# Soft-MoE weights behind attention: no dummy products in the last expert layer, finer release of weights' places, ten small products behind the last dispatch sum

## The chip, the cores and the metric

The kernel runs on one core of a Trainium2 chip. The metric is the device time of one execution in microseconds (us). Engines are named as the profile does: PE (TensorE's products; PEld its weight loads), DVE (VectorE), ACT (ScalarE), POOL (GpSimd), SP (SyncE, which issues the transfers here; SPq is its queue).

## The reference

Three layers stand behind each other, all in float32: attention with a memory term, a soft mixture of experts, and a feed-forward network. Only the second and the joint to the third matter here.

```python
x = attn_out.transpose(0, 2, 1, 3).reshape(B * S, H * D)     # 2304 tokens x 512
# soft mixture of experts: 8 experts, 4 slots each
logits = x @ phi                                             # 2304 x 32
d = softmax over tokens of logits                            # dispatch
slot_input = (d.T @ x).reshape(8, 4, 512)
for e in range(8):
    h = np.maximum(slot_input[e] @ w1[e], 0.0)               # w1[e]: 512 x 1024
    slot_out[e] = h @ w2[e]                                  # w2[e]: 1024 x 512
x = softmax over slots of logits @ slot_out                  # combine
# feed-forward: 512 -> 2048 -> 512
r = np.maximum(x @ w_in, 0.0)
out = (s * (r * r) + b) @ w_out
```

## The kernel before

The program has three stages. In the first, attention runs over 16 pairs of heads; the order of its parts is a hand-written table (`STEP`), and each batch of four pairs adds to the dispatch sum (`dispatch_sum`, L503, and `dispatch_add`, L515). While it runs, SP already loads expert weights into all the memory that is free.

The second stage is the experts. The last dispatch sum is followed by `merge`: a small product that spreads the common maximum (L537), an exponential and a multiplication (L539, L540: `sm`), a small product for the sums (L543), three small DVE steps up to the factors `sel` (L546), and four products that turn the summed tokens into slot inputs `slT` (L675, L676). Then come the expert layers in two groups of four experts: `layer1(0)`, `layer1(1)`, `layer2(0)` and, behind the combine weights, `layer2(1)`. Each product there is 32 columns wide: expert j of a group uses the strip of columns 32j to 32j+31, so that four products of different experts can run side by side. Layer 1 (L690) reads a 128 x 512 unit of `w1` for each of 4 x 2 x 4 steps, layer 2 (L706) a unit of `w2` for each of 8 x 4.

The two groups' weights are 128 units of 256 KB, 32 MB, more than there is room for. So places are used again: `load_next` requests the next weights for a place, and `used(n)` counts the units that are read and calls `load_next` for each place whose units are all done (L572). A place is two units wide in the pool `w`, or 2 to 7 units in memory that the first stage has given up (`R0`, `R1`, `R2`, `P` and others). All requests go into SP's one queue in the order of the calls; at most eight are under way, since each also waits for the landing of the eighth before it.

`layer2(1)` also has dummy products (L711): one 128 x 512 product behind each of the eight steps over `fc`, of the identity with the weights that were just read, into a scratch sum that nobody reads. Its real sum is taken out by ACT (`evac(so, acc)`, L714, recorded as L220), transposed (L717) and multiplied by `w_in` into the pieces of G (`g_piece`, L769 and L773).

The third stage runs `first` (L814 and steps on ACT and DVE) and `second` (L839 to L841, dense products) over all tokens. The output weights' first two requests (L192, into PT) wait for the last transposes of the combine weights (L753), the next one (into raw) for the last product of `layer2(1)`.

In the first stage, `warm(i)` puts small products (L216: identity with 64 columns of itself, as many as `T["wt"][i]` says) behind the parts of the last pair that the table `after` names.

Of the kernel before, what the change touches and what calls it, by code (L numbers as in the profile page):

```python
# [57 lines left out]
LEAST, MOST = struct.unpack("2f", struct.pack("2I", 896 << 20, 0x47EFFFFF))  # L58
TG = 384
T = dict(  # L60
    warm=1,
    wt=[3, 4, 4, 4, 3, 3],
    cp=['aaadaaadaaadaaad', 'aaadaaadaaadaaad', 'adadadadadadadad'],
    NB=4,
    sim=0,
# [26 lines left out]
def strided(ap, *dims):  # L92

    return bass.AP(ap.tensor, ap.offset, [list(ap.ap[0])] + [list(d) for d in dims])
# [3 lines left out]
def tile_attention_moe_ffn(  # L98
# [16 lines left out]
    PE, ACT, DVE, POOL, SP = nc.tensor, nc.scalar, nc.vector, nc.gpsimd, nc.sync  # L115
# [6 lines left out]
    ident = cs[:, L_ID:L_ID + 128]  # L122
# [30 lines left out]
    wt = {}  # L153
# [64 lines left out]
    def evac(dst, src, eng=None):  # L218
        if eng is None or eng == "n":
            nc.any.tensor_copy(dst, src)  # L220
        elif eng == "a":
            ACT.activation(out=dst, in_=src, func=AF.Copy)  # L222
        else:
            DVE.tensor_copy(dst, src)
# [340 lines left out]
    def load_next(place_of=None):  # L565

        n, tag = place_of or next(places, (0, None))
        if n and wnext[0] < len(wkeys):
            load_place(n, tag)
            held.append((wnext[0], n, tag))  # L570

    def used(n):  # L572
        freed[0] += n
        while held and held[0][0] <= freed[0]:
            _, n, tag = held.pop(0)
            if tag not in ONCE:
                load_next((n, tag))
# [23 lines left out]
    for name in SHARED:  # L601
# [1 line left out]
    batch = {  # L603
        "dx": (dispatch_exp, 0), "de": (dispatch_exp, 1), "dT": (dispatch_T, 0), "dU": (dispatch_T, 1),
        "gT": (slot_logits, 0), "gU": (slot_logits, 1), "ds": (dispatch_sum,), "du": (dispatch_add,)}
    after = {"V4": 0, "A": 1, "X": 2, "L": 3, "de": 4, "dT": 5}

    def part_of(name, p):
        if name in batch:
# [57 lines left out]
    def ps_h():  # L667
        return pH.tile([128, 512], F32, tag="h", name="h")

    def ps_y():  # L670
        return pY.tile([128, 512], F32, tag="y", name="y")
# [13 lines left out]
    def layer1(a):  # L685
        acc = [ps_y(), ps_y()]
        for kc in range(4):
            for fb in range(2):
                for j in range(4):
                    PE.matmul(  # L690
                        acc[fb][32 * j:32 * j + 32, :], slT[:, kc, :], wt["w1", a, kc, j, fb],
                        start=(kc == 0), stop=(kc == 3))
            used(8)
        for fb in range(2):
            ACT.activation(out=hs[:, fb * 512:(fb + 1) * 512], in_=acc[fb], func=AF.Relu)
        for g in range(2):
            t = ps_h()
            for i in range(4):
                PE.transpose(t[:, i * 128:(i + 1) * 128], hs[:, (4 * g + i) * 128:(4 * g + i + 1) * 128], ident)
            evac(hT[a][:, 4 * g:4 * g + 4, :], t.rearrange("p (i s) -> p i s", i=4))  # L700

    def layer2(a):
        acc = ps_y()
        for fc in range(8):
            for j in range(4):
                last_pe[0] = PE.matmul(  # L706
                    acc[32 * j:32 * j + 32, :], hT[a][:, fc, 32 * j:32 * j + 32], wt["w2", a, fc, j],
                    start=(fc == 0), stop=(fc == 7))
            if a == 1 and T["warm"]:
                for _ in range(T["warm"]):  # L710
                    PE.matmul(scratch, ident, wt["w2", a, fc, 0], start=True, stop=True)  # L711
            if fc % 2:
                used(8)
        evac(so, acc)  # L714
        t = ps_h()
        for dc in range(4):
            PE.transpose(t[:, dc * 128:(dc + 1) * 128], so[:, dc * 128:(dc + 1) * 128], ident)  # L717
        evac(sT[:, :, 16 * a:16 * a + 16].rearrange("p c (j s) -> p c j s", j=4),
             strided(t[:, 16 * a:16 * a + 1], (128, 4), (36, 4), (1, 4)))

    layer1(0)
    layer1(1)
    layer2(0)
    scratch = ps_y()


    XC = place("x", SIZE["x"], F32R)
# [3 lines left out]
    for b in range(B):  # L731
# [22 lines left out]
        evac(cT[:, b * S + 512:(b + 1) * S], t[:, 0:64])  # L754

    layer2(1)

    RC = [place(f"R{i}", SIZE[f"R{i}"], F32R) for i in range(3)]
# [167 lines left out]
```

## Time and profile before

| | |
|---|---|
| median of 3 runs | 505.52 us (504.72 to 506.94) |
| the profiled execution, its own time | 507.53 us |
| its span, first to last instruction | 505.7 us |
| mean granted clock of TensorE | 0.99 |
| PE busy | 478.2 us, 95% |
| DVE, ACT busy | 316.0 and 316.4 us |

The median is what the changed kernel's time is set against. The profiled execution is another, single run; all times of views below count from its first instruction. The granted clock is a share of 2.4 GHz: 1.00 is that, 0.50 is 1.2 GHz.

### The profile page before, as it was taken

The page shows a single profiled execution, that of the slowest core. Times are in us where ns is not written, and L with a number is a line of the kernel's source. Part 1 is how long each engine was busy: PE and PEld are TensorE (multiplying, and loading weights), DVE is VectorE, ACT ScalarE, POOL GpSimd, SP SyncE. Part 2 cuts the span into 40 slices and gives each one's busy share as a digit, 9 for nine tenths or more (in the row PEclk, how much of TensorE's full clock was granted, in tenths as well). Part 3 has the DMA queues.
Part 4 walks back from the last instruction along what each step waited for, and adds up shares of the span by engine and source line. Part 5 has one row for each costly group of instructions (what it writes and reads, how often), then busy time and mean ns, then how long its engine had stood idle before and what let it go on. Part 6 is the DMA issues. An engine that isn't in the chain of part 4 may idle for free.

```text
span 505.7 us, 12512 instructions
## 1 busy us (share of the span) xinstructions
PE 478.2 (95%) x5043; PEld 347.3 (69%) x5043; DVE 316.0 (62%) x830; ACT 316.4 (63%) x611; POOL 47.3 (9%) x90
## 2 busy tenths in 40 slices
PE   6989998979998999889997999999999999999997
PEld 3667676757676768633322578878888888888885
DVE  3869786949796977500604899873654645545451
ACT  3968685848685956103205999996755655556552
POOL 3230404130403041000000000000000000000000
PEclk9999999989999999979999999999999999999999
DMA  8883746453746464989982334200300100100001
GB/s 249 246 248 102 224 147 182 160 166 107 220 149 179 168 234 162 393 300 387 387 310 83 106 145 167 84 0 1 125 2 0 62 1 0 64 0 33 31 1 62
DMA packets 40281, 71.91 MB, mean 142 GB/s; under 512 B 4000, under 2 KB 16800, under 8 KB 40224
## 3 DMA queue, kind: packets, MB, share of 16 engines
q1 hardware_dynamic: 39072, 70.51, 41.3%
q8 instruction: 40, 0.66, 0.5%
q10 hardware_dynamic: 1152, 0.60, 0.5%
q14 instruction: 17, 0.14, 0.1%
HBM read 66.38 MB, written 4.72 MB: 141 GB/s over the span
## 4 chain that ended last, share of the span: by engine, by line
PE 89%; ACT 5%; issue 3%; DVE 2%; DMA 1%; DVEq 0%; ACTq 0%
PE y L841 13%; PE y L839 13%; PE y L840 13%; PE s L401 10%; PE s L370 8%; PE s L323 8%; PE y L706 4%; PE h L814 3%; PE y L690 3%; ACT P L361 2%; PE s L386 2%; PE y L711 2%; PE s L336 2%; PE s L439 1%; ACT PT L222 1%
## 5 line engine op out<-in xcount | busy, mean ns | idle before, releaser
L841 PE MATMUL y<-w,R 128*128 128x512 f32 x288 | 113.9, 395 | 0.0
L840 PE MATMUL y<-w,R 128*128 128x512 f32 x288 | 113.8, 395 | 0.0
L839 PE MATMUL y<-w,R 128*128 128x512 f32 x288 | 112.9, 394 | 0.9 <-ACT R L822 0.9
L361 ACT ACTIVATE P<-P,st 128x384 f32<-128x384 f32 (+3 forms) x144 | 75.8, 577 | 16.3 <-DVE st L345 15.6
L818 ACT ACTIVATE P<-h 128x384 f32<-128x384 f32 x96 | 46.7, 488 | 56.3 <-PE h L814 56.1
L823 DVE TENSOR_TENSOR R<-P,R 128x384 fp32r<-128x384 f32 x56 | 31.1, 556 | 68.3 <-ACT R L822 68.2
L222 ACT ACTIVATE PT<-s 128x768 f32<-128x768 f32 (+1 forms) x64 | 50.3, 819 | 31.5 <-PE s L370 31.4
L345 DVE CUSTOM_DVE_ANT_0 P<-s,cs 128x384 f32<-128x384 f32 (+3 forms) x128 | 57.2, 485 | 13.3 <-PE s L323 12.9
L839 PEld LDWEIGHTS y<-w,R 128*128 128x128 f32 x288 | 54.0, 188 | 16.2 <-ACT R L822 1.8
L841 PEld LDWEIGHTS y<-w,R 128*128 128x128 f32 x288 | 54.1, 188 | 13.4 <-issue 0.5
L840 PEld LDWEIGHTS y<-w,R 128*128 128x128 f32 x288 | 54.0, 188 | 9.1 <-issue 0.2
L370 PE MATMUL s<-cs,P 128*128 128x128 f32 x392 | 51.6, 278 | 1.3 <-ACT PT L222 0.8
L370 PEld LDWEIGHTS s<-cs,P 128*128 128x128 f32 x392 | 41.9, 141 | 12.3 <-issue 7.6
L821 ACT ACTIVATE P<-P,sbt 128x384 f32<-128x384 f32 x56 | 39.8, 710 | 1.5
L814 PE MATMUL h<-x,R 128*128 128x384 f32 x96 | 33.3, 349 | 0.6 <-ACT P L818 0.6
L401 PE MATMUL s<-raw,PT 128*64 128x65 f32 x768 | 28.3, 229 | 4.7 <-issue 4.7
L401 PE MATMUL s<-Q,PT 128*64 128x65 f32 x768 | 28.6, 224 | 4.4 <-issue 4.4
L401 PEld LDWEIGHTS s<-Q,PT 128*64 128x64 f32 x768 | 24.9, 137 | 11.0 <-issue 9.9
L433 POOL TENSOR_TENSOR x<-x,R 128x512 f32<-128x512 f32 (+1 forms) x15 | 21.1, 1409 | 120.0 <-DVE R L419 88.8
L401 PEld LDWEIGHTS s<-raw,PT 128*64 128x64 f32 x768 | 25.3, 142 | 9.7 <-issue 9.1
L820 ACT ACTIVATE P<-P 128x384 f32<-128x384 f32 x56 | 29.5, 526 | 1.5
L822 ACT ACTIVATE R<-P 128x384 fp32r<-128x384 f32 x56 | 29.4, 524 | 1.3
(192 smaller groups left out, 659.2 us busy)
## 6 DMA issues: line engine op xcount, KB each, us to landing
w<-in_w_dram SPq DMA_DIRECT2D x37, 512.0 KB, 6.5
raw<-in_w_in_dram SPq DMA_DIRECT2D x8, 1024.0 KB, 5.2
R<-in_qk_dram SPq DMA_DIRECT2D x32, 144.0 KB, 3.9
out_dram<-P SPq DMA_DIRECT2D x18, 256.0 KB, 2.1
raw<-in_w_out_dram SPq DMA_DIRECT2D x4, 1024.0 KB, 4.9
R<-in_w_dram SPq DMA_DIRECT2D x6, 512.0 KB, 8.9
P<-in_w_dram SPq DMA_DIRECT2D x6, 512.0 KB, 9.0
PT<-in_w_out_dram SPq DMA_DIRECT2D x3, 1024.0 KB, 4.9
```

The source lines that it names most:

```text
L222: ACT.activation(out=dst, in_=src, func=AF.Copy)
L323: PE.matmul(s_t[p, t][h][HALF[a], :], q[r, t * 128 + 64 * a:t * 128 + 64 * a + 64], k[r, 0:n], start=True, stop=True)
L345: DVE.tensor_tensor_reduce(out=Pt[t][:, n * h:n * h + n], in0=s_t[p, t][h], in1=cs[:, L_END - n:L_END], scale=-0.125, scalar=BIG, op0=ALU. ...
L361: ACT.activation(out=pt, in_=pt, func=AF.Exp, scale=-1.0, bias=st[:, c:c + 1])
L370: PE.transpose(tp[:, j * 128:(j + 1) * 128], PA[:, c:c + 128], ident)
L401: PE.matmul(o[HALF[a], 512 * h + 65 * t:512 * h + 65 * t + 65], PT[t][:, c + 64 * a:c + 64 * a + 64], v[:, v0:v0 + 65], start=(kb == 0), s ...
L814: PE.matmul(hp[:, 0:TG], G(k * 128, 128), cT[:, g * TG:(g + 1) * TG], start=True, stop=True)
L818: ACT.activation(out=r, in_=hp[:, 0:TG], func=AF.Relu)
L821: ACT.activation(out=r, in_=r, func=AF.Identity, scale=sbt[:, 0:1], bias=sbt[:, 1:2])
L839: PE.matmul(acc[g, i], hi[:, c], who[k], start=(k == 0), stop=False)
L840: PE.matmul(acc[g, i], hi[:, c], wlo[k], start=False, stop=False)
L841: PE.matmul(acc[g, i], lo[:, c], who[k], start=False, stop=(k == NK - 1))
```

## The change

Three edits. The dummy products of `layer2(1)` and their scratch sum go. `used(8)` behind each full step becomes `used(2)` behind each pair of units. And `warm` gets a seventh entry: ten small products behind the last pair's `ds`, which is `dispatch_sum` with `merge(1)` (the product L537) at its end.

```diff
 T = dict(
-    warm=1,
-    wt=[3, 4, 4, 4, 3, 3],
+    wt=[3, 4, 4, 4, 3, 3, 10],
...
-    after = {"V4": 0, "A": 1, "X": 2, "L": 3, "de": 4, "dT": 5}
+    after = {"V4": 0, "A": 1, "X": 2, "L": 3, "de": 4, "dT": 5, "ds": 6}
...
                         start=(kc == 0), stop=(kc == 3))
-            used(8)
+                    if fb:
+                        used(2)
...
-            if a == 1 and T["warm"]:
-                for _ in range(T["warm"]):
-                    PE.matmul(scratch, ident, wt["w2", a, fc, 0], start=True, stop=True)
-            if fc % 2:
-                used(8)
+                if fc % 2:
+                    used(2)
...
-    scratch = ps_y()
```

**First place**, on PE, from the last dispatch sum to the first expert layer (s and h are sums in PSUM, Es the dispatch weights, M's row the maxima, cs the constants with the identity). Before:

```order
L506 MATMUL s<-x,Es 32x512 x4
L510 MATMUL s<-x,Es 32x128 x4
L537 MATMUL s<-cs,M 128x1
L543 MATMUL s<-sm,cs 128x1
L675 MATMUL h<-sel,uacc 128x32 x4
```

and now, with line numbers one lower:

```order
L505 MATMUL s<-x,Es 32x512 x4
L509 MATMUL s<-x,Es 32x128 x4
L536 MATMUL s<-cs,M 128x1
L215 MATMUL s<-cs 128x64 x10
L542 MATMUL s<-sm,cs 128x1
L674 MATMUL h<-sel,uacc 128x32 x4
```

The ten products stand between the product of the maxima and the product of the sums, in PE's queue ahead of the latter.

**Second place**, on PE, the last half of `layer2(1)` (y is its sum; w, R and P are places of weights, raw the hidden values; the row with the dummies has cs, the identity). Before:

```order
L711 MATMUL y<-R_3459,cs 128x512
L711 MATMUL y<-R_3470,cs 128x512
L706 MATMUL y<-R_3470,raw 32x512
L706 MATMUL y<-P,raw 32x512 x2
L706 MATMUL y<-R_3470,raw 32x512 x2
L706 MATMUL y<-P,raw 32x512 x4
L711 MATMUL y<-P,cs 128x512 x2
L706 MATMUL y<-R_3517,raw 32x512
L706 MATMUL y<-w,raw 32x512
L706 MATMUL y<-P,raw 32x512
L706 MATMUL y<-R_3517,raw 32x512 x2
L706 MATMUL y<-w,raw 32x512
```

and now:

```order
L706 MATMUL y<-R_3480,raw 32x512
L706 MATMUL y<-P,raw 32x512 x2
L706 MATMUL y<-R_3480,raw 32x512 x2
L706 MATMUL y<-P,raw 32x512 x4
L706 MATMUL y<-R_3528,raw 32x512
L706 MATMUL y<-w,raw 32x512
L706 MATMUL y<-P,raw 32x512
L706 MATMUL y<-R_3528,raw 32x512 x2
L706 MATMUL y<-w,raw 32x512
```

The real products stand in the same order, without the dummies between them; the same holds for the four dummies further ahead.

**Third place**, on SP, the first requests for used places in layer 1, with the semaphores that each waits for (DMAHW: an earlier landing; PE: a product). Before:

```order
L173 DMA M<-in_w_dram 128x2x512 [waits DMAHW1_49,PE_49,Activation_49]
L173 DMA w<-in_w_dram 128x2x512 [waits DMAHW2_49,PE_49]
L173 DMA w<-in_w_dram 128x2x512 [waits DMAHW3_49,PE_49]
L173 DMA w<-in_w_dram 128x2x512 [waits DMAHW4_49,PE_49]
L173 DMA w<-in_w_dram 128x2x512 [waits DMAHW5_49,PE_49]
```

and now:

```order
L172 DMA M<-in_w_dram 128x2x512 [waits DMAHW1_49,PE_49,Activation_49]
L172 DMA w<-in_w_dram 128x2x512 [waits DMAHW2_49,PE_49]
L172 DMA w<-in_w_dram 128x2x512 [waits DMAHW3_49,PE_49]
L172 DMA w<-in_w_dram 128x2x512 [waits DMAHW4_49,PE_49]
L172 DMA w<-in_w_dram 128x2x512 [waits DMAHW5_49,PE_49]
```

Nothing moved here, nor in the rest of SP's 216 rows.

## Rows read from the trace of the kernel before

**Rows 1.** The page: busy time of each engine.

```profile
PE 478.2 (95%) x5043; PEld 347.3 (69%) x5043; DVE 316.0 (62%) x830; ACT 316.4 (63%) x611; POOL 47.3 (9%) x90
```

**Rows 2.** Windows: length, PE, PEld, DVE, ACT, POOL busy, clock, DMA share, GB/s.

```profile
210.00:215.00 5.00, 4.14 (x38) 2.70 (x36) 2.05 (x9) 2.25 (x11) 0.00 (x0) 1.00 1.01 394
215.00:220.00 5.00, 3.58 (x17) 2.18 (x20) 1.07 (x5) 0.00 (x0) 0.00 (x0) 0.54 1.05 390
220.00:225.00 5.00, 5.00 (x40) 1.31 (x36) 0.00 (x0) 0.00 (x0) 0.00 (x0) 0.77 0.53 152
225.00:230.00 5.00, 5.00 (x52) 1.44 (x48) 0.00 (x0) 0.00 (x0) 0.00 (x0) 1.00 1.05 400
...
260.00:262.00 2.00, 2.00 (x16) 0.47 (x15) 0.00 (x0) 0.00 (x0) 0.00 (x0) 1.00 1.03 402
262.00:264.00 2.00, 2.00 (x10) 0.76 (x12) 0.00 (x0) 0.00 (x0) 0.00 (x0) 1.00 0.44 170
264.00:270.00 6.00, 6.00 (x34) 1.55 (x28) 0.00 (x0) 0.00 (x0) 0.00 (x0) 1.00 0.00 1
270.00:275.00 5.00, 3.60 (x34) 1.93 (x33) 3.14 (x7) 3.42 (x9) 0.00 (x0) 1.00 0.63 210
...
280.00:285.00 5.00, 5.00 (x24) 2.71 (x23) 3.93 (x6) 4.95 (x9) 0.00 (x0) 1.00 0.40 162
```

**Rows 3.** Chain of waits, 246 to 283: shares by line; start, us, what.

```profile
by line: PE y L706 34.1%; PE y L711 21.8%; PE h L750 5.1%; PE h L773 4.2%; ACT raw L220 3.8%; PE h L717 3.6%; PE y L839 3.2%; issue 3.0%; ACT P L820 2.8%; ACT P L818 2.7%; PE h L769 2.4%; PE h L753 2.2%; PE y L841 1.9%; PE h L814 1.9%; PE y
...
262.01 1.91 PE y L711 x4
...
266.61 1.91 PE y L711 x4
268.53 1.89 PE y L706 x12
...
270.50 0.59 ACT raw L220
```

**Rows 4.** SP's last two weight requests: issue (start) and us to landing.

```profile
L173 SPq DMA_DIRECT2D R<-in_w_dram x1: 378/378/378, 252.0 to 252.0; - x1
...
DMA to landing us min/median/max: 8.8/8.8/8.8
L173 SPq DMA_DIRECT2D w<-in_w_dram x1: 379/379/379, 252.8 to 252.8; - x1
...
DMA to landing us min/median/max: 9.4/9.4/9.4
```

**Rows 5.** Timeline, 202 to 226: start, length, engine, line, operation, records [idle before].

```profile
208.82 0.97 PEld L216 LDWEIGHTS s<-cs 128*128 128x128 f32 x8
...
209.88 0.75 PEld L216 LDWEIGHTS s<-cs 128*128 128x128 f32 x6
...
213.49 0.38 PE L537 MATMUL s<-cs,M 1*128 1x1 f32 x2
...
214.43 0.16 DVE L540 TENSOR_TENSOR sm<-sm,ssum 128x1 f32<-128x1 f32 x1 [0.36 <-ACT sm L539]
...
214.64 0.38 PE L543 MATMUL s<-sm,cs 128*128 128x1 f32 x2 [0.77 <-DVE sm L540]
...
215.99 1.89 PE L675 MATMUL h<-sel,uacc 128*128 128x32 f32 x8 [0.97 <-DVE sel L546]
...
218.33 8.14 PE L690 MATMUL y<-w,slT 128*32 128x512 f32 x56 [0.45 <-DVE slT L676]
219.19 0.20 PEld L690 LDWEIGHTS y<-w,slT 128*32 128x32 f32 x4 [0.66 <-issue]
220.04 0.20 PEld L690 LDWEIGHTS y<-w,slT 128*32 128x32 f32 x4 [0.66 <-issue]
...
221.98 4.21 SPq L173 DMA_DIRECT2D w<-in_w_dram  x8
...
222.87 0.12 PEld L690 LDWEIGHTS y<-w,slT 128*32 128x32 f32 x4 [0.31 <-issue]
```

## Prediction

> **What bounds the kernel now.** The page comes first: TensorE is busy for 95% of the span [rows 1], so time is won or lost on PE, and only where PE's work is not needed or comes too late. Stage by stage [rows 2], the reader is to look at two columns, the granted clock and the DMA share. Up to 262 the transfers run at a full share (1.03 in 260 to 262), with one hole, 220 to 225, where the share is 0.53. Behind 264 they stand still (0.00 in 264 to 270) while PE is 100% busy: there PE alone decides. The clock is at 1.00 (the 2.4 GHz level) everywhere here but in two rows: mean 0.54 in 215 to 220 and 0.77 in 220 to 225, a spell at 1.2 GHz.
>
> The chain of waits says what PE does behind 246 [rows 3]: of the 37 us from 246 to 283, 21.8% are the dummy products of L711, 8.07 us. They are on the chain itself. The last ones run from 262.01 (1.91 us, two dummies) and from 266.61 (1.91 us, two more), then comes the last piece of the second expert layer, 1.89 us from 268.53, and at 270.50 ACT takes the sum out.
>
> What would PE wait for if they were gone? The weights' requests [rows 4]: the last one leaves SP at 252.8 and lands 9.4 us later, at 262.2; the one before it leaves at 252.0 and lands after 8.8, at 260.8.
>
> **Edit 1, no dummies.** PE's own work would end at 270.42 - 8.07 = 262.35 if no weight were late. But the last weights (the last w of the order) land at 262.2, and two of the last six products read them. In the new order [the change, second place] these six are the same that make up the last piece of the chain, 12 records (a product stands as two in the trace: L675's four are x8 there) in 1.89 us [rows 3]. The second of the six waits for the last landing, the four behind it stand in PE's queue, the sixth reads the same weights in the same strip of columns. So the layer ends between 262.2 + 1.7 (two products of one strip behind each other, of 2 x 0.43 us each by the spacing of L690's records [rows 5]) and 262.2 + 1.9 (the whole piece); I take 264.1. ACT's evacuation moves from 270.50 to 264.2: **-6.3 us**. The first 1.8 us of the dummies' 8.07 are thus lost to a new wait, for weights. The bound above is the whole 8.07 (no wait at all), the bound below is the clock's (rivals). What comes next does not depend on an absolute time: the output weights' first two requests are out before the layer's end, the next one waits for this layer's last product, so it moves along; and from 280 PE is fully busy again [rows 2].
>
> **Edit 2, places given back by two units.** Here I reckon 0. A request waits for the product that last read its place, not for the call that gives the place back; the call only says where the request stands in SP's queue. SP's order is the same row by row, its waits too [the change, third place], and in the built program each of these waits stands on the same product as before (its count is ten higher for the ten new ones). Above 0 it could only cost if a request were moved past another; none is. The order also swaps three small DVE rows in the combine weights (a reduction to 5 columns, two casts), which I take as free too: DVE has nothing at all to do in 260 to 270 [rows 2], so whatever they delay is caught up before PE's last weights are there.
>
> **Edit 3, ten small products behind the last dispatch sum.** They stand between L537 and L543 on PE [the change, first place]. Their price: four such products took 0.97 us of weight loads, three took 0.75 [rows 5], so 0.245 us each and 2.45 us for ten. L537 ends at 213.87, so they run to 216.3. L543 started at 214.64, held by DVE's sm (L540, to 214.59); now it waits for PE until about 216.35: 1.7 us later, and behind it in a row the three DVE steps to sel, the slot products L675 and all of layer 1. This is the new cost. What it may buy is the clock: L675 took 1.89 us and the first groups of four records of L690 came 0.85 us apart (219.19 to 220.04) against 0.43 later (0.31 idle and 0.12 busy at 222.87) [rows 5], the two levels of the clock. The first weight request behind the hole waits for the fifth product of L690 and left at 221.98.
> - If the clock holds: L675 starts at 217.65 and takes 0.95, L690 starts at 218.33 + 1.7 - 0.95 = 219.1, and the fifth product ends half of (221.98 - 218.33) = 1.8 us later, at 220.9: the request leaves **1.1 us earlier**.
> - If the clock falls just when L690 starts: 219.1 + 3.65 = 222.7, **0.8 us later**.
>
> Before the clock fell, PE had only L543 and L675 to do from 213.87 to 218.33, 4.5 us; now that thin stretch runs from 216.3 to 219.1, 2.8 us, with ten products ahead of it. No row says on which side it falls. The middle of the two is -0.15; I take **-0.3 us**, nearer to the gain, since the stretch is the shorter one (range -1.1 to +0.8). From 225 on, the stream runs at a full share (1.05 in 225 to 230) [rows 2], so it moves as a whole and the last landing with it; the hole (47% of 5 us, 2.3 us) leaves room for that. If the request leaves 0.8 later, the end of edit 1 goes to 264.9.
>
> **The sum.** -6.3 + 0 - 0.3 = -6.6 us. The profiled execution took 507.53 us itself (505.7 of span and 1.8 around it), which would go to 500.9. It was 2.0 us above the median of the runs, 505.52; from the median the forecast is **498.9 us**.
>
> **The rivals.**
> - *The clock falls while PE waits for the last weights.* For: behind 256 PE, without dummies, has one lone product (a quarter of the columns) per landing and then waits about a microsecond for the next; the trace shows such a fall after thin work, 215 to 222. Against: PE kept the clock in 270 to 275 with 3.60 us busy of 5, and in 210 to 215 with 4.14 [rows 2]. Price: the last piece goes from 1.89 to 3.7 (+1.8), and the pieces of G behind it, PE's 3.60 us of 270 to 275, take up to 3.6 more; much of that stretch is a chain through ACT, so I take +2.6. That leaves 6.6 - 4.4 = 2.2 of the gain: **503.3 us**.
> - The Trainium skill, in "TensorE: Matmul & The Clock Gate", section "HAM oscillation — how this bites in real kernels", says that a kernel whose bursts of products are shorter than the waits for transfers between them is throttled anew at each wait. By that rule this rival's 503.3 is the time and not 498.9. The fall at 215 agrees with the rule in kind (work too thin), but no run here shows PE waiting in bursts for weights.
> - *Slower.* The same fall, but the clock stays at 1.2 GHz into the second layer's dense products. To end more than 2.5 us above before it must cost 6.6 + 2.5 = 9.1: 1.8 + 3.6 = 5.4 up to there, and 3.7 more, so the dense products (5.00 us busy of 5 in 280 to 285) must stay slow for 7.4 us. Place: from 273 to 281 of the new run. That gives **508.1 us**. Against: L690 began at 218.33 at 1.2 GHz, and the mean of 0.77 over 220 to 225 says that only 2.3 us of these were slow, so that dense work brought the clock back at 222.3, 4 us after its start [rows 2, 5].
> - *The dummies were hidden anyway.* If PE had to wait for weights as long as the dummies took, nothing but edit 3 would remain: **505.2 us**. Against: the landing at 262.2 and the idle transfers from 264 on. It would need a stream that ends 6 us later than before.
>
> **How the numbers follow.** The forecast has 0.60, the fallen clock 0.28, the slower one 0.05, the hidden dummies 0.07. The forecast's own range is 497.0 (the stream 1.1 earlier, and a microsecond for the spread of the runs) to 501.0 (0.8 later and the same spread). To leave out no more than 2 in 10 the range must take in most of the fallen clock: **497.0 to 504.6**. Half a per cent, 2.5 us, is about what a measurement of this kernel tells from no change; faster means below 503.0. All of the forecast and half of the fallen clock lie there: 0.74. Slower 0.05, the rest, 0.21, is no change.
>
> **What would show it.** Right: no rows of L711; DMA full until about 262, ACT's evacuation of the sum (L220 behind L706) at 264 instead of 270.5, directly behind the last landing; idle time on PE named by weights in 256 to 262; the span 6 to 7 us shorter and every stretch behind 270 unchanged in length. For edit 3, L543 at about 216.3, and the first w request of L173 at 221 or at 222.7, according to the clock in 216 to 222. For edit 2, the requests in the same order. Wrong: a granted clock below 1.00 anywhere in 256 to 280, with the pieces of G stretched; or the last weights landing later than 263.

## The result, and the profile after

The changed kernel took **501.5 us** (median of 20 runs, 496.5 to 506.7). The kernel before, run in the same set, took 508.12 us there (20 runs, 504.1 to 514.7). The ratio is **0.9889, 95% interval 0.9862 to 0.9916**: 1.1% faster, and of the 505.52 us of the three runs shown it makes 499.9 us, 5.6 us less. The forecast was 6.6 us less. The ratios and intervals in this document leave out each kernel's slow runs, those more than 1.5% above its fastest (three of the changed kernel's 20 here), so they are not quotients of the medians beside them, which would give 0.987 here.

The profiled execution is one that TensorE's clock disturbed early: it took 506.7 us, with three falls of the clock in the first stage. So spans are not compared here but stretches, counted from the end of the product of the maxima, the last product ahead of the place of the ten new ones. It is L537 in the kernel before and L536 in the changed one, whose lines are numbered one lower; below it is called L537 for every kernel. The page's first line for the changed kernel answers to [rows 1] (a product is two records: 16 of the dummies are gone, 20 of the ten small products have come, 5043 to 5047):

```profile
PE 475.3 (94%) x5047; PEld 349.1 (69%) x5047; DVE 315.9 (63%) x830; ACT 316.4 (63%) x611; POOL 47.2 (9%) x90
```

The windows of the changed kernel, 218 to 275, answer to [rows 2] (its L537 ends at 217.84 and not at 213.87, so these lie some 4 us later):

```profile
218.00:222.00 4.00, 3.12 (x29) 3.07 (x28) 1.48 (x6) 0.65 (x3) 0.00 (x0) 0.99 1.05 387
222.00:225.00 3.00, 2.55 (x15) 0.99 (x18) 0.29 (x1) 0.00 (x0) 0.00 (x0) 0.50 0.92 337
225.00:230.00 5.00, 5.00 (x32) 1.15 (x28) 0.00 (x0) 0.00 (x0) 0.00 (x0) 0.62 0.43 123
230.00:235.00 5.00, 5.00 (x52) 1.43 (x48) 0.00 (x0) 0.00 (x0) 0.00 (x0) 1.00 1.04 395
255.00:260.00 5.00, 4.91 (x27) 1.94 (x25) 3.06 (x10) 1.65 (x5) 0.00 (x0) 1.00 1.05 387
...
264.00:267.20 3.20, 1.96 (x6) 0.14 (x2) 0.00 (x0) 0.00 (x0) 0.00 (x0) 1.00 1.02 396
267.20:269.20 2.00, 1.90 (x10) 0.38 (x10) 0.00 (x0) 0.00 (x0) 0.00 (x0) 1.00 0.22 86
269.20:275.00 5.80, 3.89 (x36) 2.32 (x36) 4.40 (x9) 4.57 (x13) 0.00 (x0) 1.00 0.51 181
```

Read them from the bottom. The transfers run at a full share until 267.2 and PE's last piece ends 2 us later; the six microseconds of [rows 2] in which the transfers stood still while PE was 100% busy are gone. In 264 to 267.2 PE is busy for 1.96 of 3.20 us, and the clock is 1.00 all the same. Further up, the clock is low for some 7 us: 0.50 over the 3 us from 222, and 0.62 over the next 5, so 3.8 of these. It fell at 222, behind the ten products and 1 us ahead of the start of the first expert layer (222.98 in the chain below).

The chain of waits of the changed kernel, 217 to 270, answers to [rows 3]:

```profile
217.54 0.31 PE s L536 x2
217.84 2.37 PE s L215 x20
...
221.27 1.28 PE h L674 x8
222.64 0.30 DVE slT L675
222.98 13.15 PE y L689 x93
236.13 10.78 DMA w<-in_w_dram
246.98 10.75 DMA R<-in_w_dram
257.79 9.38 DMA w<-in_w_dram
267.21 1.92 PE y L706 x10
269.21 0.59 ACT raw L219
```

The dummies' place on the chain has been taken by transfers: three requests, each waiting for an earlier one's landing, the last of them out at 257.79 and landed 9.38 us later, at 267.17. PE starts its last piece 0.04 behind that, and ACT takes the sum out 2.04 behind it. The timeline of the changed kernel names the new wait (start, length, engine, line, records, in brackets the idle time and its releaser):

```profile
265.86 1.04 PE L706 MATMUL y<-R,raw 128*32 128x512 f32 x2 [0.95 <-DMA R<-in_w_dram]
267.21 0.62 PE L706 MATMUL y<-w,raw 128*32 128x512 f32 x1 [0.31 <-DMA w<-in_w_dram]
```

The first used place is requested at 226.63 in the same timeline, 8.79 us behind L537; before it was 8.11 [rows 5]:

```profile
226.63 5.29 SPq L172 DMA_DIRECT2D w<-in_w_dram  x9
```

So the path from L537 to ACT's evacuation is 269.21 - 217.84 = 51.37 us, against 270.50 - 213.87 = 56.63 before: 5.26 less. The span fell by only 0.8 us (505.74 to 504.94), because L537 itself came 3.97 us later in this execution and the stretch behind the evacuation was 0.48 longer; 3.97 - 5.26 + 0.48 = -0.81.

### The profile page after: what moved, and what is told of

The parts are those of the page before. It is cut to its first block, busy times and chain, and to the rows that moved or that the text cites. A ratio compares the mean times of both kernels' runs of the same rounds, so it can differ in the third digit from the quotient of the medians.

```text
span 504.9 us, 12520 instructions
## 1 busy us (share of the span) xinstructions
PE 475.3 (94%) x5047; PEld 349.1 (69%) x5047; DVE 315.9 (63%) x830; ACT 316.4 (63%) x611; POOL 47.2 (9%) x90
## 4 chain that ended last, share of the span: by engine, by line
PE 80%; DMA 8%; ACT 5%; issue 3%; DVE 2%; DVEq 0%; ACTq 0%; SPq 0%
PE y L837 13%; PE y L835 12%; PE y L836 12%; PE s L400 10%; PE s L369 8%; PE s L322 8%; DMA w<-in_w_dram 4%; PE h L810 3%; PE y L689 3%; DMA R<-in_w_dram 2%; ACT P L360 2%; PE s L385 2%; PE s L335 2%; PE s L438 1%; DMA raw<-in_w_out_dram 1%
## 5 line engine op out<-in xcount | busy, mean ns | idle before, releaser
L400 PE MATMUL s<-Q,PT 128*64 128x65 f32 x768 | 29.8, 230 | 5.0 <-issue 5.0
L400 PEld LDWEIGHTS s<-Q,PT 128*64 128x64 f32 x768 | 26.1, 142 | 11.8 <-issue 10.7
```

The source lines that it names most:

```text
L400: PE.matmul(o[HALF[a], 512 * h + 65 * t:512 * h + 65 * t + 65], PT[t][:, c + 64 * a:c + 64 * a + 64], v[:, v0:v0 + 65], start=(kb == 0), s ...
```

## The experiments

My theory after the result: edit 1 (no dummies) is the whole gain; edit 2 (finer release) is nothing; edit 3 (the ten products) costs, since they come ahead of the sums' product and the clock falls anyway. The rivals: edit 3 buys clock and edit 1 gives less than it seems; or edit 2 moves something that the order doesn't show. Runs in one set share one chip and its runs of the kernel before; there were three sets. The first held no_dummies, ten_alone, by_two_alone and fitted (median of before 507.17), the second two_dummies, fewer_weights, changed_again and fitted_again (506.97), the third no_dummies_again, changed_third, fitted_third and full_width (506.90). Ratios are compared within a set; the rows of the table below come from all three.

A single table carries the traces, one profiled execution per row. Each number is a difference of two rows of that execution's timeline: from the end of L537 to the first weight request for a used place (**request**), to the landing of the last weights (**landing**), from there to ACT's evacuation of the second layer's sum (**behind**), and the whole of it (**path**); then L537's own end, and the stretch from the evacuation to the end of the span (**rest**). All in us.

| kernel, execution | request | landing | behind | path | L537 ends | rest |
|---|---|---|---|---|---|---|
| before | 8.11 | 48.32 | 8.31 | 56.63 | 213.87 | 235.25 |
| by_two_alone | 8.12 | 48.71 | 8.00 | 56.71 | 215.75 | 234.85 |
| ten_alone | 8.98 | 49.42 | 8.80 | 58.22 | 209.93 | 235.69 |
| two_dummies | 7.19 | 47.56 | 19.05 | 66.61 | 213.27 | 236.37 |
| no_dummies | 7.17 | 48.33 | 2.04 | 50.36 | 211.23 | 234.87 |
| no_dummies_again | 7.15 | 47.69 | 2.04 | 49.73 | 212.53 | 236.25 |
| the change | 8.79 | 49.33 | 2.04 | 51.37 | 217.84 | 235.73 |
| changed_again | 8.47 | 49.00 | 2.04 | 51.03 | 212.79 | 236.29 |
| changed_third | 8.08 | 48.54 | 2.04 | 50.58 | 212.61 | 234.86 |
| full_width | 7.85 | 48.24 | 2.04 | 50.28 | 219.33 | 235.53 |
| fitted | 5.56 | 46.47 | 2.04 | 48.51 | 212.05 | 234.86 |
| fitted_again | 5.56 | 46.84 | 2.04 | 48.88 | 217.80 | 236.37 |
| fitted_third | 5.56 | 45.94 | 2.04 | 47.98 | 212.23 | 234.86 |
| fewer_weights | 9.24 | 44.18 | 3.76 | 47.93 | 213.80 | 239.55 |

**Edit 1 alone** (no_dummies, no_dummies_again). Against the changed kernel:

```diff
-    wt=[3, 4, 4, 4, 3, 3, 10],
+    wt=[3, 4, 4, 4, 3, 3],
...
-    after = {"V4": 0, "A": 1, "X": 2, "L": 3, "de": 4, "dT": 5, "ds": 6}
+    after = {"V4": 0, "A": 1, "X": 2, "L": 3, "de": 4, "dT": 5}
...
-                    if fb:
-                        used(2)
+            used(8)
...
-                if fc % 2:
-                    used(2)
+            if fc % 2:
+                used(8)
```

> Edit 1 alone: the eight dummy products go, the rest is as before. My theory: the layer ends 1.9 us behind the last weights' landing, ACT takes the sum out 2.0 to 2.1 us behind that landing (8.3 before), so this edit is nearly the whole gain: -6.3 us, ratio 0.9875, and PE has idle time named by weights. Rival, the clock falls while PE waits for weights: a granted clock below 1.00 between the last landing and the first second-layer product, and only 2 us gained, ratio 0.996. Rival, the ten small products carry the change: nothing gained here.

> Edit 1 alone once more, beside the change and the fitted products on one chip. By the traces so far the last weights land 47.6 to 48.7 us behind the product of the maxima in kernels without the ten products and 49.0 to 49.4 with them. Theory: edit 1 alone is about 1 us faster than the whole change. Rival: the ten products gain in runs that were not profiled, the whole change is as fast or faster.

Measured: 499.2 us, ratio 0.984 (0.9786 to 0.9895); the second time 502.24 us, 0.9922 (0.9894 to 0.995). The chain of waits of no_dummies ends as that of the whole change does, with the last weights:

```profile
250.14 9.41 DMA w<-in_w_dram
...
259.60 1.92 PE y L705 x10
...
261.59 0.59 ACT raw L219
```

In the traces, behind goes from 8.31 and 8.00 to 2.04 both times, and the mean path from 56.67 (before and by_two_alone) to 50.05: -6.6 us. Of these, 6.1 stand in behind; the other 0.5 is an earlier landing, in executions where the clock stayed low for some 3 us around the start of the first layer and not for some 7. So edit 1 is the gain. But the two ratios of one and the same kernel hardly meet; a pair of medians does not tell this kernel from the whole change, whose ratios lie between them.

**The ten products alone** (ten_alone) and **the finer release alone** (by_two_alone). Against before:

```diff
-    wt=[3, 4, 4, 4, 3, 3],
+    wt=[3, 4, 4, 4, 3, 3, 10],
...
-    after = {"V4": 0, "A": 1, "X": 2, "L": 3, "de": 4, "dT": 5}
+    after = {"V4": 0, "A": 1, "X": 2, "L": 3, "de": 4, "dT": 5, "ds": 6}
```

```diff
-            used(8)
+                    if fb:
+                        used(2)
...
-            if fc % 2:
-                used(8)
+                if fc % 2:
+                    used(2)
```

> Edit 3 alone: ten small products behind the last dispatch sum, dummies stay. Theory: 2.4 us of products, L543 1.7 us later; the first weight request leaves 9.1 us behind the end of the product of the maxima if the clock falls at the start of the expert layers (8.4 before) and 7.3 if it holds. The end of the layer is then set by PE's dummies, not by the weights, so the whole moves with the start of layer 1: between 1 us earlier and 1 us later, ratio 0.998 to 1.002. Rival, the products keep the clock and are worth it: faster by over 0.3%. Rival, pure delay: 1.7 us slower, 1.0034.

> Edit 2 alone: places given back by two units. Theory: the same instructions in the same order with the same waits, so ratio 1.000, and what it differs from 1.000 is what this measurement tells of noise. Rival, earlier requests: the hole behind the last request of the first stage is shorter and the stream ends earlier, up to 2 us.

Measured: 508.21 us, ratio 1.0015 (0.9975 to 1.0055), and 508.48 us, 1.0015 (0.9974 to 1.0056). The finer release leaves the order of the instructions as it was, so its ratio is also a measurement of nothing: half a per cent either way is what these runs can't tell. (The three DVE rows that the prediction puts under edit 2 belong to edit 1: DVE's 830 instructions stand in the old order in by_two_alone and in the new one in no_dummies.) The ten products lie within that too; only the trace shows their price. The windows of ten_alone from 210 (its L537 ends at 209.93):

```profile
210.00:214.00 4.00, 3.12 (x28) 3.07 (x28) 1.57 (x6) 0.65 (x3) 0.00 (x0) 0.98 1.04 388
214.00:220.00 6.00, 5.55 (x28) 1.85 (x32) 0.29 (x1) 0.00 (x0) 0.00 (x0) 0.50 0.61 214
220.00:225.00 5.00, 5.00 (x48) 1.40 (x44) 0.00 (x0) 0.00 (x0) 0.00 (x0) 0.93 0.98 336
```

The clock holds through the ten products, is low for the whole of 214 to 220, on the second half of the slot products and the first expert layer, and is back before 221. Over the four executions with the ten products (ten_alone and the three of the change) the last landing lies 49.07 us behind L537 in the mean (48.54 to 49.42), over the five without them or a substitute (before, by_two_alone, two_dummies, and the two without dummies) 48.12 (47.56 to 48.71): by these means the edit costs 0.95 us. The ranges touch, since the clock's low spell at this place was short (some 3 us) in some executions of either group and long (some 7) in others. At equal spells they part: with a short one the request leaves 8.47 and 8.08 behind L537 with the ten products against 7.15 to 7.19 without, with a long one 8.98 and 8.79 against 8.11 and 8.12. That is 1.1 and 0.8 later in the mean.

**Two dummies per step** (two_dummies), against before:

```diff
-    warm=1,
+    warm=2,
```

> The kernel before with two dummy products behind each step instead of one. Theory: from the second half of the layer on the dummies are on the path one behind the other, 1.0 us each, so eight more push ACT's evacuation from 8.3 us behind the last landing to 15.5 to 16.5 us. Rival, dummies run in time in which PE would wait anyway: under 2 us more.

Measured: 518.03 us, one run, 11.1 above the median of 506.97 before. Behind grows from 8.31 to 19.05, by 10.7 us, where eight more dummies at the price of the first eight would be 8.07. The chain of waits of two_dummies, at its end, says why:

```profile
275.92 0.98 PE y L706 x2
276.90 1.06 PE y L711 x2
277.95 1.85 PE y L706 x10
...
279.88 0.59 ACT raw L220
```

A lone real product with a dummy on each side takes 0.98, while the five products of the last piece (ten records) take 1.85 together. So a dummy costs its own time and also pulls apart products that would have run side by side. Nothing swallowed any of the added time: the layer's end was on the path as read. This kernel and the next, fewer_weights, were run once each, so their totals have no interval.

**Fewer weights** (fewer_weights). The loads of the last eight units of `w2` are left out, and the second group's last two steps multiply with the weights of two steps earlier; the work on PE is the same. Against the changed kernel:

```diff
+    wkeys = wkeys[:-8]
...
-                    acc[32 * j:32 * j + 32, :], hT[a][:, fc, 32 * j:32 * j + 32], wt["w2", a, fc, j],
+                    acc[32 * j:32 * j + 32, :], hT[a][:, fc, 32 * j:32 * j + 32], wt["w2", a, fc - 2 if a and fc > 5 else fc, j],
```

> The changed kernel without the last eight units of the second experts' weights: they are not requested, and the last two steps of the last layer multiply with the weights of the two steps ahead of them, so the output is another. Theory, the end of the layer waits for the last landing alone: the stream ends five requests and 5.4 us earlier, and the layer's end follows until PE's own work binds, so ACT takes the sum out 3 to 4 us earlier, counted from the first weight request (42.6 us in the profiled run of the change, 39 to 39.5 here), and at 3.5 to 4.5 us behind the last landing instead of 2.0. Rival, PE's own products bind already: counted from the request no change.

Measured: 503.15 us, one run, with behind at 3.76: the layer ends 3.76 behind its last landing, not 2. From the request to the evacuation it is 47.93 - 9.24 = 38.7 us, against 42.6 in the changed kernel and 48.5 before. So the weights cost the changed kernel 3.9 us, and PE's own work without dummies is 9.8 us shorter by these executions, not 8.07. The total did not follow: rest is 239.55, against 234.9 to 236.4 everywhere else, some 3 to 5 us more. The windows of fewer_weights show one part of it:

```profile
260.00:265.00 5.00, 3.22 (x37) 1.21 (x27) 3.15 (x7) 2.88 (x6) 0.00 (x0) 1.00 0.43 147
265.00:270.00 5.00, 4.37 (x20) 2.31 (x24) 3.37 (x7) 3.31 (x10) 0.00 (x0) 0.52 0.51 170
270.00:275.00 5.00, 4.83 (x16) 2.49 (x8) 1.12 (x2) 4.92 (x8) 0.00 (x0) 0.50 0.30 124
```

The clock falls to the 1.2 GHz level at 265, behind the evacuation at 261.7, in the pieces of G, and stays there until 275. The other part stands in its chain of waits, which goes past the layer's end, through the first output weights (PT):

```profile
255.86 0.22 PE h L750
256.10 4.88 DMA PT<-in_w_out_dram
261.00 0.69 ACT Q L201
...
264.09 0.05 ACT w L799
...
264.62 0.27 ACT raw L222
```

Their request waits for the last transposes of the combine weights (L750), which this experiment leaves where they were (the request is 33.1 us behind the first weight request, 33.5 in the changed kernel). With the layer's end nearer to them, ACT takes out the first piece of G (L222) behind a step of their decoding (L799): 2.89 us behind the evacuation of the layer's sum, against 2.09 in changed_third. So the output weights are the next wait behind the experts' weights, and an earlier end of the layer alone would not be paid back in full. How much of the 3 to 5 us is this and how much the clock, this one execution doesn't part.

**Two products that fit the gaps** (fitted, fitted_again, fitted_third). The ten products are replaced by one of 352 columns behind `ds` and one of 448 behind `du`, where PE waits for DVE anyway. Against the changed kernel, from which the ten go:

```diff
+    FIT = {"ds": 352, "du": 448}
...
+        if p == NPAIR - 1 and name in FIT:
+            PE.matmul(bank_pair()[:, 0:FIT[name]], ident, cs[:, 0:FIT[name]], start=True, stop=True)
```

> As changed, but for the ten small products: one product of 352 columns behind the product of the maxima and one of 448 behind the product of the sums, each in a stretch where PE waits anyway (0.77 and 0.97 us). Theory: no delay on the way to layer 1, and the full-width products hold the clock through the first expert products more often; the first weight request leaves 6.2 to 6.6 us behind the end of the product of the maxima if it holds (8.4 before, 9.1 in the profiled run of the change), 8.4 if it does not. Against the kernel before -6.3 to -8.1 us, ratio 0.984 to 0.9875. Rival, the clock falls all the same: the gain is edit 1's alone, 0.9875.

> The fitted products once more beside the change on one chip. Theory: the request leaves 5.6 to 6.6 us behind the product of the maxima, so the whole is 1.5 to 3 us faster than the changed kernel, ratio to before 0.982 to 0.985. Rival, the clock does not hold in other runs: the same time as the changed kernel within half a per cent, with a request 8 us behind.

> The fitted products, third look. Theory: the last landing 46.4 to 46.9 us behind the product of the maxima, 2.4 us ahead of the change, so 0.3 to 0.6% faster than it. Rival: within 0.2% of the change.

Measured: 499.57, 499.51 and 501.17 us; ratios 0.9843 (0.9783 to 0.9903), 0.9842 (0.9794 to 0.9889) and 0.9821 (0.9782 to 0.986). The timeline of PE in fitted:

```profile
211.67 0.38 PE L536 MATMUL s<-cs,M 1*128 1x1 f32 x2
211.98 0.86 PE L620 MATMUL s<-cs 128*128 128x352 f32 x2
212.82 0.38 PE L542 MATMUL s<-sm,cs 128*128 128x1 f32 x2
213.07 1.00 PE L620 MATMUL s<-cs 128*128 128x448 f32 x2
214.18 1.05 PE L678 MATMUL h<-sel,uacc 128*128 128x32 f32 x8
215.68 6.64 PE L693 MATMUL y<-w,slT 128*32 128x512 f32 x60 [0.45 <-DVE slT L679]
```

The product of the sums (L542) starts 0.77 behind the end of L537 (212.05), as in the kernel before, where it was 0.77 too [rows 5]; the slot products start 0.11 behind the second filler. The first expert layer starts 3.63 us behind L537, exactly as in no_dummies: the fillers delay nothing. Then the clock, in the windows of fitted:

```profile
215.00:220.00 5.00, 4.55 (x44) 1.45 (x47) 0.29 (x1) 0.00 (x0) 0.00 (x0) 1.00 1.03 363
220.00:225.00 5.00, 5.00 (x52) 1.56 (x48) 0.00 (x0) 0.00 (x0) 0.00 (x0) 1.00 1.03 381
```

It stays at 1.00, the hole in the transfers is gone (1.03 and 1.03), and the request leaves 5.56 behind L537 in all three executions, 2.5 to 3.2 us earlier than in the change. The last landing comes 46.4 us behind L537 in the mean, 2.5 before that of the change (49.0) and 1.6 before that of edit 1 alone (48.0). The totals do not show this gain clear of the noise. In the one set that held all three kernels, fitted's interval (0.9782 to 0.986) lies clear of those of no_dummies_again and changed_third (0.9894 upward), but it rests on the three fastest of its six runs; the median of all six, 501.17 us, is only 0.2% under those two (502.24 and 501.95). In the other two sets the intervals overlap, and in the first, fitted and edit 1 alone have the same ratio (0.9843 and 0.984).

**Wide products in one place** (full_width): three products of 512, 512 and 384 columns where the ten stood.

```diff
+    FIT = {"ds": (512, 512, 384)}
```

> As changed, but the ten products of 64 columns are three of 512, 512 and 384 columns in the same place, 2.35 us against 2.37: the same delay with PE's columns full. If the ten were too thin to hold the clock, it holds here, L690's first request leaves 7.0 to 7.4 us behind the product of the maxima and the last weights land at 48 us. If the empty stretch behind them brings the clock down whatever they are, the request leaves at 8.5 to 9.2 and the landing is at 49.0 to 49.4.

Measured: 502.01 us, ratio 0.9875 (0.9835 to 0.9915). This one settles little: in the execution profiled, the clock had already fallen, eleven microseconds ahead of L537's end, and then it fell once more. The windows of full_width (L537 ends at 219.33):

```profile
210.00:215.00 5.00, 5.00 (x44) 4.68 (x45) 1.39 (x6) 1.01 (x5) 0.00 (x0) 0.50 1.04 407
215.00:220.00 5.00, 5.00 (x31) 3.06 (x31) 1.12 (x6) 1.01 (x5) 0.00 (x0) 0.65 1.05 390
220.00:225.00 5.00, 3.67 (x23) 2.21 (x25) 1.62 (x6) 0.23 (x2) 0.00 (x0) 1.00 0.49 176
225.00:230.00 5.00, 5.00 (x40) 1.29 (x32) 0.00 (x0) 0.00 (x0) 0.00 (x0) 0.66 0.35 80
```

What it does show is that wide products in the place of the ten delay the sums' product as the ten do (it starts 2.40 us behind L537, 2.21 with the ten and 0.77 without), and that one execution with them had the low clock in the first expert layer too (0.66 over 225 to 230). The request at 7.85 and the landing at 48.24 lie between the two forecasts of the expectation.

**The change again** (changed_again, changed_third), unaltered, beside the others of its set:

> The changed kernel once more, for a second look at the clock behind the ten small products. Theory: the clock falls again near the start of layer 1, the first weight request leaves 8.8 to 9.1 us behind the end of the product of the maxima; ACT takes the sum out 2.0 us behind the last landing; ratio 0.987. Rival, the look before was bad luck in phase: the clock holds and the request leaves 7.3 us behind.

> The change, third look. Theory: the last landing 49.0 to 49.4 us behind the product of the maxima, ACT's evacuation 2.0 us behind the landing, ratio 0.986 to 0.989. Rival: a landing at 48 us, clock at 1.00 through the first expert products.

Measured: 501.32 us, ratio 0.9868 (0.9825 to 0.9911), and 501.95 us, 0.9922 (0.9896 to 0.9948), the same ratio as edit 1 alone in that set. The three profiled executions of the change put its path at 51.37, 51.03 and 50.58; edit 1 alone, in the third one's set, stands at 49.73, 0.85 less.

## Why the prediction came out as it did

**The direction, and nearly the size, were right**: 6.6 us less forecast, 5.6 less measured (4.2 to 7.0 by the interval). The traces' own sum is -6.6 for edit 1 and +0.95 for edit 3, -5.7. The 1.0 us between forecast and result lies within the interval, so the runs alone would not call any term wrong; the traces do. That the total fits so well is in part luck: edit 1 gave 0.3 more than its term, with the shorter low spell of the clock in its executions, and hides part of what edit 3 missed.

**What bounds the kernel: right.** The dummies were on the path [rows 3], the transfers had ended long before [rows 2, 4], and taking the dummies out moved the evacuation.

**Edit 1, -6.3: right.** The layer now ends with the weights: the last piece starts 0.04 us behind the last landing, takes 1.92 (I had 1.7 to 1.9), and the evacuation stands 2.04 behind the landing in every execution without dummies that loads all the weights, nine of nine. What the working got too small is "PE's own work would end at 270.42 - 8.07 = 262.35 if no weight were late": a dummy also breaks up products that run side by side, and fewer_weights puts PE's own work at 9.8 less. It did not matter for the sum, since the weights set the end either way; it makes the loss to the new wait 3.9 us and not 1.8. The bound "no wait at all" leaves out the output weights, which fewer_weights shows to come next.

**Edit 2, 0: right**, as far as half a per cent can tell, and the identical order says why.

**Edit 3: here a term failed**, "I take **-0.3 us**, nearer to the gain, since the stretch is the shorter one (range -1.1 to +0.8)". It was +0.95 in the mean, at the loss end of that range and a little beyond. The delay was sized well: L542 now waits for 2.37 us of products behind L537 and is 1.45 us later than before (I had 1.7). But the clock did not hold in any of the four executions with them: it was low over 3.3 to 5.8 us of the first layer, and over 3.2 to 4.1 us in the five without. So the layer starts later (4.9 to 5.3 us behind L537, against 3.6 to 4.5) and runs at the low clock as long or longer, and the request comes 1.0 us later in the mean (8.58 against 7.55). That the thin stretch was shorter was no reason for a gain; no row stood behind that step. With its gaps filled and nothing delayed, as in fitted, the clock held in three executions of three. The kernel before was also read from one execution: its request at 8.11 is the later of two values that occur (7.15 to 7.19 in three executions), by how long the clock stayed low.

**The stream moves as a whole: right for a delay.** From the request to the last landing it is 40.2 us before, 40.6 in by_two_alone and 40.4 to 40.5 in the four executions with the ten products, so the delay of the request arrives nearly whole at the layer's end. A request that leaves earlier can lose part of that on the way: 40.5 and 41.2 in the two executions of edit 1 alone, 40.4 to 41.3 in fitted.

**The fallen clock while PE waits for weights: did not happen.** In nine executions of nine the clock is 1.00 from 255 to the evacuation, though PE is busy for only 1.96 us of 3.20 in 264 to 267.2. The kernel that the Trainium skill describes ("TensorE: Matmul & The Clock Gate", section "HAM oscillation — how this bites in real kernels") has bursts of products that are shorter than the waits between them. That case did not arise here: in the timeline above a wait of 0.95 us is followed by 1.04 us of products and a wait of 0.31 by the last piece. So these rows neither bear that section out nor contradict it, and the prediction took it further than it reaches. The prediction's sign of being wrong, a clock below 1.00 up to 280, did show behind the evacuation, in four of the nine (at 270.6, 272.2, 275.2, 276.5, each 7 to 9 us behind it). But the clock fell there in two of the four with dummies too, so it is no consequence of the new wait, and the rest of those six executions is 0.7 to 1.5 us longer than the shortest (235.5 to 236.4 against 234.9), not 2.6; that of the change's first one, without a fall there, is 0.9 longer as well.

**The span "6 to 7 us shorter": did not show** in the profiled execution, for a reason outside the change: the first stage, which is the same in both, took 4 us longer in it.

## What to carry to other kernels

Work that nobody reads costs what it adds to the chain and what it pulls apart around it (here 8.07 us of dummies and 9.8 in all), and when it goes, the next wait (here the last weights, 2.04 us ahead of the evacuation) says how much of it comes back. In this kernel a filler that was meant to hold the clock paid where the engine waits anyway and the filler is about as long as that wait: two products of 0.86 and 1.00 us in two gaps held it, ten small ones of 2.4 us in one queue place ahead of a needed product made that late and did not. Where runs of one kernel spread by 2%, compare stretches of traces from a common instruction and not spans.

## What was not expected of the hardware

The same instructions of the first stage end, at L537, anywhere between 209.9 and 219.3 us, and that goes with how often the clock fell ahead of it: no fall in ten_alone, no_dummies and fitted (209.9 to 212.1), one in seven executions (212.2 to 213.9), two in by_two_alone, fitted_again and full_width (215.8, 217.8, and 219.3 with one long one), three in the changed kernel's (217.8). That is some 2 us per fall in the mean, in a first stage that is the same in all of them; in which execution it falls, nothing seen here predicts. It is most of the spread between executions of one kernel: 5.2 of the 6.9 us between the spans of the three of the change, 5.8 of 8.0 for fitted. That is as large as the whole change.

PE was busy without a gap through the ten products of ten_alone, to 212.3, at a clock of 0.98 over 210 to 214, and the clock went to 0.50 at 213.8, 1.5 us behind them, in the stretch with the sums' product, the DVE steps and the slot products. With the two wider products of fitted, one of them inside that stretch, it stayed at 1.00. Small products that keep the engine busy by the profile were thus not enough for the clock. What is lacking in them, their size or their place, stays open: in full_width the clock fell behind wide products in the place of the ten as well, which speaks for the place, but that execution was disturbed ahead of it.
